# A 576 KB broadcast for the MLP gate moves from GpSimd's DMA queue beside the last transpose to SyncE's queue behind fc1's weights

## Chip, cores, metric

One core of a Trainium2 chip. The metric is device microseconds of one execution. The kernel before ran in 248.44 us (median of 3, 248.24 to 248.64) when the prediction was made.

## The reference, cut to what matters

```python
B, N, D = (2, 256, 1152); F = 4 * D                 # bf16 throughout
mod = (_silu(c) @ w_mod).reshape(B, 6, 1, D)
shift_a, scale_a, gate_a, shift_m, scale_m, gate_m = [mod[:, i] for i in range(6)]
...                                                  # attention, x = x + gate_a * a
h2 = _layernorm(x) * (1 + scale_m) + shift_m
m = _gelu(h2 @ w_fc1) @ w_fc2
return x + gate_m * m
```

`gate_m` is needed only when fc2's results are evicted, at the end. The kernel computes it on VectorE: it loads the sixth section of `w_mod` transposed, and multiplies it with silu(c), repeated on all 128 partitions. That repeated copy of silu(c), `s_all`, is the load that moves.

## The kernel before

Four blocks matter: the LayerNorm ahead of the MLP, whose rows are transposed by DMA; fc1's first eight column blocks, in two halves by batch; the broadcast; and what uses it.

```python
def ln2_transpose(t):                                   # four of these, SyncE's queue
    nc.sync.dma_start_transpose(hT[:, :, t * P:(t + 1) * P], xn2[t][:])
...
ln2_normalize(3, 5 * P)
ln2_transpose(3)                                        # the last one

w_f1[1] = load_panels("w_f1_1", wfc1_v, D)              # SyncE's queue, nine loads of 864 KB
w_f1[2] = load_panels("w_f1_2", wfc1_v, 2 * D)
w_f1[3] = load_panels("w_f1_3", wfc1_v, 3 * D)
w_gate_mT = wide_tile("w_gate_mT")
for r in range(0, KD, 3):
    nc.sync.dma_start_transpose(w_gate_mT[...], w_mod[...])
...                                                     # cut
MSPLIT = 8
for b in range(B):                                      # batch 0 needs transposes 0, 1; batch 1 needs 2, 3
    for m0 in range(0, MSPLIT, 2):
        pacc = acc_tile([P, 2, N], "pacc")
        for m in (m0, m0 + 1):
            for k in range(KD):
                f1_mm(pacc[:, m - m0, :], m, k, b * N, (b + 1) * N)
        if b == 0 and m0 == MSPLIT - 2:
            ln2_modulate(1)                             # nine modulations of hT, VectorE and ScalarE
        nc.scalar.activation(gT[:, m0:m0 + 2, b * N:(b + 1) * N], pacc[:], ACT.Gelu_apprx_tanh)
late = act.tile([P, NT, D], BF16, name="late", tag="x_in")   # takes the buffer of x_sb
s_all = late[:, 0:B, :]
for b in range(B):
    nc.gpsimd.dma_start(s_all[:, b, :], s_dram[b:b + 1, :].partition_broadcast(P))
...                                                     # cut
for m in range(MSPLIT, KF):                             # the other 28 column blocks, 512 wide
    ...
    if m == 14:
        dot_section(w_gate_mT, s_all, late[:, B, :], gcol)   # 18 multiply-and-sum passes on VectorE
        gate_m = gate_m_finish()
```

The program order of the text is not the time of the load. GpSimd's last work before it ends at 99.03 us, and what is left to wait for is the buffer of x_sb. The trace has the broadcast issued at 101.12 us, after 2.09 us of idling that VectorE's last LayerNorm statistics ended; the fourth transpose follows at 103.24 us.

## Time and profile before

| | before |
|---|---|
| median, three runs | 248.44 us |
| span of the trace, mean granted clock | 247.1 us, 0.993 |
| fourth transpose, issue to landing | 4.99 us |
| PE's wait ahead of fc1's batch-1 half | 2.21 us |
| stretch at half clock behind it | 3.41 us |
| dot passes start / first fc2 eviction | 145.65 / 183.89 us |

The lines behind these numbers, and how they are read, are in the prediction.

### The profile page before, as it was taken

The page shows a single profiled execution, that of the slowest core. Times are in us where ns is not written, and L with a number is a line of the kernel's source. Part 1 is how long each engine was busy: PE and PEld are TensorE (multiplying, and loading weights), DVE is VectorE, ACT ScalarE, POOL GpSimd, SP SyncE. Part 2 cuts the span into 40 slices and gives each one's busy share as a digit, 9 for nine tenths or more (in the row PEclk, how much of TensorE's full clock was granted, in tenths as well). Part 3 has the DMA queues.
Part 4 walks back from the last instruction along what each step waited for, and adds up shares of the span by engine and source line. Part 5 has one row for each costly group of instructions (what it writes and reads, how often), then busy time and mean ns, then how long its engine had stood idle before and what let it go on. Part 6 is the DMA issues. An engine that isn't in the chain of part 4 may idle for free.

```text
span 247.1 us, 3879 instructions
## 1 busy us (share of the span) xinstructions
PE 237.8 (96%) x1637; PEld 140.1 (57%) x1648; DVE 84.7 (34%) x198; ACT 65.5 (27%) x127; POOL 31.8 (13%) x48
## 2 busy tenths in 40 slices
PE   6999999999999999969999999999999999999994
PEld 2585444465666666848544444444566666666673
DVE  3752462115625768520000049997011000000001
ACT  6632350133514155752322233222000000000000
POOL 1000012000311515200000000002031222111111
PEclk9999999999999999997999999999999999999999
DMA  6999999999999951599999999996950000000000
GB/s 227 326 336 362 366 327 312 371 353 344 338 309 346 330 117 20 108 267 327 326 327 221 218 279 329 327 326 184 335 162 32 16 19 16 16 20 17 31 16 19
DMA packets 70685, 53.89 MB, mean 218 GB/s; under 512 B 18939, under 2 KB 65419, under 8 KB 70667
## 3 DMA queue, kind: packets, MB, share of 16 engines
q1 hardware_dynamic: 69776, 51.84, 71.8%
q0 software_dynamic: 864, 1.79, 2.6%
q8 instruction: 13, 0.21, 0.4%
q14 instruction: 5, 0.04, 0.0%
q10 hardware_dynamic: 27, 0.00, 0.0%
HBM read 48.08 MB, written 1.19 MB: 199 GB/s over the span
## 4 chain that ended last, share of the span: by engine, by line
PE 87%; DMA 5%; DVE 4%; ACT 1%; issue 1%; SPq 0%; DVEq 0%; ACTq 0%
PE pacc L766 29%; PE pacc L702 26%; PE pacc L503 7%; PE pacc L438 7%; PE pacc L612 5%; PE pk L253 4%; DMA w_scale_a<-in_w_mod_dram 3%; PE pk L282 2%; DMA hT<-xn 2%; PE pn L365 1%; PE ps_s L458 1%; PE pa L530 1%; DVE stats L624 1%; DVE stats L163 1%; PE pm L221 1%
## 5 line engine op out<-in xcount | busy, mean ns | idle before, releaser
L702 PE MATMUL pacc<-hT,w_f 128*128 128x512 bf16 (+1 forms) x390 | 72.1, 346 | 2.5 <-DVE hT L599 2.2
L766 PE MATMUL pacc<-w_f,gT 128*128 128x384 bf16 (+2 forms) x468 | 70.5, 314 | 0.1
L702 PEld LDWEIGHTS <-w_f 128*128 128x128 bf16 x396 | 39.5, 100 | 34.9 <-issue 2.9
L766 PEld LDWEIGHTS <-gT 128*128 128x128 bf16 x468 | 44.4, 98 | 26.2
L429 DVE SCALAR_TENSOR_TENSOR late<-w_gate_mT,late 128x1152 bf16<-128x1152 bf16 x18 | 24.4, 1358 | 36.3 <-DMA w_gate_mT<-in_w_mod_dram 35.7
L772 DVE TENSOR_TENSOR tmp<-pacc,gate 128x384 f32<-128x384 f32 (+2 forms) x13 | 6.9, 528 | 65.8 <-PE pacc L766 53.3
L743 ACT ACTIVATE gT<-pacc 128x512 bf16<-128x512 f32 x28 | 16.7, 597 | 37.7 <-PE pacc L702 36.3
L774 POOL TENSOR_TENSOR o_sb<-tmp,x 128x384 bf16<-128x384 f32 (+1 forms) x12 | 11.7, 973 | 50.8 <-DVE tmp L772 50.8
L612 PE MATMUL pacc<-w_o,big 128*128 128x384 bf16 (+2 forms) x117 | 18.1, 314 | 0.0
L503 PE MATMUL pacc<-w_v,hT 128*128 128x384 bf16 x108 | 17.9, 326 | 0.0
L438 PE MATMUL pacc<-hT,w_q 128*128 128x512 bf16 x80 | 17.6, 379 | 0.1
L612 PEld LDWEIGHTS <-big 128*128 128x128 bf16 x117 | 10.9, 98 | 7.1 <-DVE big L270 0.6
L503 PEld LDWEIGHTS <-hT 128*128 128x128 bf16 x108 | 10.4, 98 | 7.2 <-issue 0.5
L253 PE MATMUL pk<-big,w_k 128*128 128x256 bf16 (+2 forms) x88 | 13.3, 292 | 0.5 <-ACT big L240 0.4
L438 PEld LDWEIGHTS <-w_q 128*128 128x128 bf16 x81 | 7.9, 98 | 9.6
L618 POOL TENSOR_TENSOR x<-tmp,x_sb 128x384 f32<-128x384 f32 x10 | 9.1, 911 | 17.9 <-DVE tmp L617 10.8
L420 POOL DMA_DIRECT2D gates_dram<-grow x4 | 2.0, 512 | 69.3 <-DVE grow L729 69.3
L253 PEld LDWEIGHTS <-w_k 128*128 128x128 bf16 x90 | 7.5, 97 | 3.4 <-DMA w_k<-in_wqkv_dram 0.3
L617 DVE TENSOR_TENSOR tmp<-pacc,gate 128x384 f32<-128x384 f32 (+2 forms) x13 | 6.7, 519 | 4.8 <-PE pacc L612 4.7
L146 PE MATMUL pwarm<-zeros 128*128 128x512 bf16 x18 | 7.1, 560 | 1.2 <-DVE eps_t L92 1.2
L420 POOL DMA_DIRECT2D s_dram<-s_rows x4 | 2.6, 654 | 34.5 <-DVE s_rows L423 34.5
L240 ACT ACTIVATE big<-pt,scale_a 128x256 bf16<-128x256 bf16 (+1 forms) x12 | 4.6, 434 | 9.0 <-PE pt L231 7.4
(97 smaller groups left out, 151.2 us busy)
## 6 DMA issues: line engine op xcount, KB each, us to landing
w_f<-in_w_fc_dram SPq DMA_DIRECT2D x14, 864.0 KB, 11.1
w_f<-in_w_fc_dram SPq DMA_DIRECT2D x2, 2592.0 KB, 10.5
w_f<-in_w_fc_dram SPq DMA_DIRECT2D x2, 1728.0 KB, 13.2
w_shift_a<-in_w_mod_dram SPq DMA_DIRECT2D x3, 864.0 KB, 11.4
w_q<-in_wqkv_dram SPq DMA_DIRECT2D x3, 864.0 KB, 12.0
w_v<-in_wqkv_dram SPq DMA_DIRECT2D x3, 864.0 KB, 10.5
w_gate_a<-in_w_mod_dram SPq DMA_DIRECT2D x3, 864.0 KB, 9.9
w_o<-in_wo_dram SPq DMA_DIRECT2D x3, 864.0 KB, 13.8
```

Of the source, the lines that this page charges most:

```text
L146: nc.tensor.matmul(dst[:], zeros[:, 0:P], zeros[:], start=True, stop=True)
L253: nc.tensor.matmul(pk[m][:, c0:c1], w_k[:, k, m * P:(m + 1) * P], hT0[:, k, c0:c1], start=(k == 0 and c0 == 0), stop=(k == KD - 1), skip_g ...
L429: nc.vector.scalar_tensor_tensor(spill, wT[:, j, :], 1.0, s_all[:, b, :], op0=ALU.mult, op1=ALU.mult, accum_out=dst[:, b * KD + j:b * KD + ...
L438: nc.tensor.matmul(pacc[:], w_q[:, k, m * P:(m + 1) * P], hT[:, k, :], start=(k == 0), stop=(k == KD - 1),)
L503: nc.tensor.matmul(pacc[:], hT[:, k, t * P:(t + 1) * P], w_v[:, k, pnl * PW:(pnl + 1) * PW], start=(k == 0), stop=(k == KD - 1),)
L612: nc.tensor.matmul(pacc[:], aT[:, k, t * P:(t + 1) * P], w_o[:, k, c0:c1], start=(k == 0), stop=(k == KD - 1),)
L618: (nc.gpsimd if i < 2 or t % TPB == 0 else nc.vector).tensor_tensor(x1[:, t, c0:c1], tmp[:], x_sb[:, t, c0:c1], op=ALU.add)
L702: nc.tensor.matmul(dst, w_f1[m // KD][:, k, ml * P:(ml + 1) * P], hT[:, k, c0:c1], start=(k == 0), stop=(k == KD - 1),)
L743: nc.scalar.activation(gT[:, m, :], pacc[:], ACT.Gelu_apprx_tanh)
L766: nc.tensor.matmul(pacc[:], gT[:, kk, t * P:(t + 1) * P], w_f2[j][:, r, c0 - n * PW:c0 - n * PW + cw], start=(kk == 0), stop=(kk == KF - 1),)
L772: nc.vector.tensor_tensor(tmp[:], pacc[:], gate_m[:, b, c0:c0 + cw], op=ALU.mult)
L774: (nc.vector if last else nc.gpsimd).tensor_tensor(o_sb[:], tmp[:], x1[:, t, c0:c0 + cw], op=ALU.add)
```

## The change

The intent is to take the broadcast's traffic away from the transpose that PE waits for, and to put it where PE waits for nothing that comes by DMA. SyncE issues its DMAs in program order, so there it comes behind fc1's last weights.

```diff
     w_f1[3] = load_panels("w_f1_3", wfc1_v, 3 * D)
+    late = act.tile([P, NT, D], BF16, name="late", tag="x_in")
+    s_all = late[:, 0:B, :]
+    for b in range(B):
+        nc.sync.dma_start(s_all[:, b, :], s_dram[b:b + 1, :].partition_broadcast(P))
     w_gate_mT = wide_tile("w_gate_mT")
@@ behind fc1's two halves
-    late = act.tile([P, NT, D], BF16, name="late", tag="x_in")
-    s_all = late[:, 0:B, :]
-    for b in range(B):
-        nc.gpsimd.dma_start(s_all[:, b, :], s_dram[b:b + 1, :].partition_broadcast(P))
```

## The prediction

> **What bounds the kernel now.** I read the page's first and fourth parts first: TensorE matmuls are busy 96% of the 247.1 us span and 87% of the chain that ended last is PE, so a change to a 576 KB load can only matter where PE waits for it, directly or through something that it slows. The slices of the page have one place where the granted clock falls, the eighteenth to nineteenth (about 111 to 117 us).
>
> ```profile
> PE 237.8 (96%) x1637; PEld 140.1 (57%) x1648; DVE 84.7 (34%) x198; ACT 65.5 (27%) x127; POOL 31.8 (13%) x48
> PEclk9999999999999999997999999999999999999999
> ```
>
> Then the waits of PE: the longest of the whole kernel is a single one of 2.2 us in front of fc1's second half (batch 1, line 702), released by the modulation of hT on VectorE. The chain in order of time says what lies behind it.
>
> ```profile
> 102.29 0.93 ACT xn L577
> 103.22 0.02 issue
> 103.24 4.99 DMA hT<-xn
> ...
> 108.32 0.36 DVE hT L599
> 108.68 0.04 issue
> 108.72 10.42 PE pacc L702 x73
> ```
>
> So the last of the four DMA transposes of the normalised rows is on the path, 4.99 us from issue to landing. The view of the tile hT gives all four; at least two, and by the view of the DMA queues in short stretches three, took 3.2 us:
>
> ```profile
> DMA to landing us min/median/max: 3.2/3.2/5.0
> ```
>
> The timelines of GpSimd and PE around it show what ran beside the slow one, and the hole:
>
> ```profile
> 101.12 1.08 POOL L721 DMA_DIRECT2D late<-s_dram  x2 [2.09 <-DVE stats L624]
> ```
> ```profile
> 98.48 8.02 PE L702 MATMUL pacc<-hT,w_f 128*128 128x256 bf16 x72
> 108.72 3.68 PE L702 MATMUL pacc<-hT,w_f 128*128 128x256 bf16 x19 [2.21 <-DVE hT L599]
> ```
>
> The two broadcasts of 288 KB are issued at 101.1 and 101.7 and land 5.2 and 5.5 us later, at about 106.4 and 107.2. In quarter-microsecond windows the DMA engines fall back at 102.75 (the third transpose's bytes are through), then stay at 110 to 280 GB/s until 106.5. The fourth transpose, issued at 103.24, moves its bytes in the middle of that. The third, issued at 100.28, was done as the broadcast's bytes began, and took 3.2 us. That is the evidence that the broadcast is what costs the fourth 1.8 us.
>
> The hole has a second price. Windows of PE behind it:
>
> ```profile
> 108.72:110.34 1.62, 1.62 (x11) 0.97 (x11) 1.23 (x5) 1.62 (x4) 0.00 (x0) 1.00 1.08 332
> 110.34:113.75 3.41, 3.41 (x19) 2.35 (x17) 0.00 (x0) 0.63 (x2) 0.00 (x0) 0.51 1.09 328
> 113.75:119.14 5.39, 5.39 (x48) 4.67 (x48) 0.00 (x0) 1.37 (x3) 0.00 (x0) 1.00 1.10 326
> ```
>
> The columns are the stretch, its length, busy time and count of PE, weight loads, VectorE, ScalarE and GpSimd, then the granted clock. For 3.41 us the clock is half. The second half of this stage (73 matmuls) thus takes 10.42 us, where 72 of the first half took 8.02, or 8.13 for 73: 2.29 us longer, of which 3.41 x 0.5 = 1.71 is the clock and the remaining 0.58 the start at the pace of the nine modulations.
>
> **What the Trainium skill says.** "DMA: Bandwidth & Descriptors", section "Issuing engines are not separate DMA queues": transfers started by GpSimd, Sync or Scalar all run on the same 16 DMA engines and interleave. The trace agrees: a transpose on SyncE's queue took 4.99 instead of 3.2 us beside GpSimd's load. The same page, "DMA Transpose (X-bar)" and "Rules for kernel authors": a transpose next to ordinary DMAs needs no serialising, so I expect no new forced wait from putting the broadcast directly ahead of the gate's transposes; no run of before has that order. "TensorE: Matmul & The Clock Gate", Part 1: the clock gate watches PE activity in free-running windows of 3413 ns and drops to half after an idle window. The trace agrees with the length (3.41 us at half clock) and with the half, but it differs on the condition: the idle stretch was 2.21 us, not a whole window, and was followed by a thinly filled start. So what counts seems to be how full a window was, and the measurement decides.
>
> **The change part by part.** The instruction order of the changed program shows the same instructions on every engine but for two: GpSimd loses the two broadcasts, and SyncE has them between fc1's fourth quarter and the three transposes of w_gate_mT. PE, VectorE and ScalarE keep their order. The two copies wait there for the writers of s_dram, for x_sb's last reader on GpSimd, and for older transfers that share their semaphores, all long past.
> - *Removed:* the traffic beside the fourth transpose. It then should take what the other three do, 3.2 us: 103.24 + 3.2 = 106.44 instead of 108.22, 1.79 us less. The first modulation follows 0.10 later and takes 0.36, then 0.04 to PE: 106.94. PE ends the first half at 98.48 + 8.02 = 106.50, so the hole shrinks from 2.21 to 0.43 us. It doesn't close, so the whole 1.79 us are gained on the path.
> - *The clock:* with a hole of 0.43 and the 0.58 of the paced start, a window of 3.41 us loses about 1.0 us and is some 70% filled. Before, the worst window (107.00 to 110.41) had PE busy for 1.69 of 3.41 us, 50%, and was followed by the drop. The start of the kernel has thin windows too: 10.00 to 13.41 has 2.66 of 3.41, 78%, without a drop. The new 70% lies between; I put 85% on no drop. Gain if so: 1.71 us; expected 1.45.
> - *Added on SyncE's queue:* 2 x 288 KB, some 590 kB at the 327 GB/s that the loads run at, 1.8 us of the DMA engines around 127 us. The gate's transposes (issued from 127.25 on), the dot passes that wait for them (145.65) and fc2's first loads (143.60) move back by up to about 2 us. Is any of it on the path? First use of the gate: the dot passes start at 145.65 and the first fc2 eviction at 183.89, 38.24 us behind, so it moves to some 186.
>
> ```profile
> 145.65 1.36 DVE L429 SCALAR_TENSOR_TENSOR late<-w_gate_mT,late 128x1152 bf16<-128x1152 bf16 x1 [35.70 <-DMA w_gate_mT<-in_w_mod_dram]
> 183.89 0.56 DVE L772 TENSOR_TENSOR tmp<-pacc,gate 128x384 f32<-128x384 f32 x1 [12.59 <-DMA gate<-gates_dram]
> ```
>
> PE has six accumulators and needs 70.47 / 12 = 5.87 us for one group of fc2, so from a start at 169.6 it would first stall at 169.6 + 6 x 5.87 = 204.9: 19 us of slack. VectorE catches up at 0.56 us a group, GpSimd at about 1.0. fc2's first weights, issued at 143.60, take 10.6 us (landing 154.2), the second panel's about 13 (near 160); 2 us later both are still 7 us or more ahead of 169.6. None of this is on the path.
> - *Sum:* 1.79 + 1.71 = 3.50 us when both come, 1.79 when the clock still drops. 248.44 - 3.50 = 244.94; weighted, 248.44 - 1.79 - 1.45 = 245.2. I take 245.1.
>
> **The rivals.**
> 1. *The clock drops all the same.* The windows are free-running, so how the hole lies in them can decide. For it: 70% is below the fullest thin window that I can show as harmless. The time would be 246.6.
> 2. *w_fc1's second quarter takes the broadcast's place.* Its loads are issued behind the fourth transpose at 104.63, and bytes follow about 1.1 us after an issue here (transpose issued 90.64, engines active from 91.75): from 105.75. The undisturbed transpose moves its bytes from about 104.35 to 106.0, so the overlap is 0.3 us or so. If the slow 4.99 us were mostly this load's doing, the gain would be a few tenths: 248.0. Against it: the engines are visibly at work from 103 on, before those loads are even issued. A partial overlap, landing at 3.6 us, costs 0.4: 245.4.
> 3. *The gate comes late, or fc2's weights do.* SyncE's queue is in order, so a copy that had to wait would hold back the transposes and all fc2 loads behind it. The slack of 7 and 19 us speaks against it; it would need a wait of over 7 us to show, and then the time would exceed 248.4.
>
> **Range and chances.** Both gains give 244.9, a partly disturbed transpose without the drop 245.4, the drop 246.6 to 247. Runs of before lie within 0.2 us of the median. Eight in ten: 244.4 to 246.9. The gain can't reach the 2% line (243.47) unless more than hole and clock went: the two together, hole closed, are 2.21 + 1.71 = 3.92, leaving 244.5. Faster by over 2%: 0.02; slower: 0.01; within: 0.97.
>
> **What would show it.** Right: the fourth transpose lands in 3.2 to 3.6 us; PE's wait ahead of the second half is 0.4 to 0.8 us; no window at half clock near 110 us; fc1's full-width part starts near 115.7 instead of 119.19; the dot passes start 0 to 2.5 us later, PE never waits in fc2. Wrong: a transpose that still takes about 5 us (rival 2), a half clock behind a short hole (rival 1), or a wait of PE at line 766 or for w_fc1 panels (rival 3).

## The result, and the profile after

The changed kernel took 245.33 us (median of 4, 245.28 to 246.9) against 248.54 us (median of 4) for the kernel before; the ratio is 0.9887, 95% interval 0.9847 to 0.9928. (A ratio is the mean time of one kernel's fast runs over that of the other's fast runs of the same rounds, so not quite the ratio of the medians.) The change is a gain of 1.1%, real but within the 2% line.

First the chain in order of time of the kernel after: start, duration, what.

```profile
103.68 0.93 ACT xn L577
104.61 0.02 issue
104.63 3.29 DMA hT<-xn
...
108.02 0.36 DVE hT L599
108.37 0.04 issue
108.41 8.76 PE pacc L706 x73
```

The fourth transpose takes 3.29 instead of 4.99 us, and the 73 matmuls behind it 8.76 instead of 10.42. The timeline of PE has the hole shrunk from 2.21 to 0.50 us, and the windows behind it stay at full clock (columns as in the prediction):

```profile
99.89 8.02 PE L706 MATMUL pacc<-hT,w_f 128*128 128x256 bf16 x72
108.41 11.78 PE L706 MATMUL pacc<-hT,w_f 128*128 128x256 bf16 x86 [0.50 <-DVE hT L599]
```
```profile
110.03:113.44 3.41, 3.41 (x34) 3.05 (x32) 0.00 (x0) 1.01 (x3) 0.00 (x0) 1.00 1.10 332
```

In these 3.41 us 31 matmuls began where 16 began before (the views' counts, 34 and 19, take in the three that were already running).

One thing must not be read as an effect of the change. All times in this trace up to the hole are 1.4 us later than before (fc1 starts at 99.89, not 98.48): this profiled run was the 246.9 us one, and its slices of granted clock show why:

```profile
PEclk9889999999999999999999999999999999999999
```

The clock fell early, at about 10 to 14 us, in code that is the same in both kernels, behind a PE wait of 1.2 us for the first weights. The other three runs had mean granted clocks of 0.998 to 1.0 and took 245.3. So in the first four runs each, after had a half clock in one run of four, at another place; before had one in its profiled run and, by their times (248.2 us and more, see below), in the other three, whose clocks are not listed. Comparing two traces by absolute time would hide 1.4 us of the gain; comparing each stage by its own length does not.

### The profile page after: what moved, and what is told of

It is laid out like the page before. It is cut to its first block, busy times and chain, and to the rows that moved or that the text cites. A ratio compares the mean times of both kernels' runs of the same rounds, so it can differ in the third digit from the quotient of the medians.

```text
span 245.0 us, 3884 instructions
## 1 busy us (share of the span) xinstructions
PE 237.3 (97%) x1637; PEld 140.3 (57%) x1648; DVE 84.5 (34%) x198; ACT 65.5 (27%) x127; POOL 30.7 (13%) x46
## 4 chain that ended last, share of the span: by engine, by line
PE 89%; DMA 4%; DVE 4%; issue 1%; ACT 1%; SPq 0%; DVEq 0%; ACTq 0%
PE pacc L766 29%; PE pacc L706 25%; PE pacc L503 7%; PE pacc L438 7%; PE pacc L612 6%; PE pk L253 5%; DMA w_scale_a<-in_w_mod_dram 3%; PE pk L282 2%; PE pn L365 1%; PE ps_s L458 1%; PE pa L530 1%; DMA hT<-xn 1%; PE pt L231 1%; DVE stats L624 1%; PE pm L221 1%
## 5 line engine op out<-in xcount | busy, mean ns | idle before, releaser
L706 PE MATMUL pacc<-hT,w_f 128*128 128x512 bf16 (+1 forms) x390 | 70.5, 340 | 0.8 <-DVE hT L599 0.5
L706 PEld LDWEIGHTS <-w_f 128*128 128x128 bf16 x396 | 38.6, 98 | 32.4 <-issue 1.2
L253 PE MATMUL pk<-big,w_k 128*128 128x256 bf16 (+2 forms) x88 | 14.2, 311 | 0.5 <-ACT big L240 0.4
L253 PEld LDWEIGHTS <-w_k 128*128 128x128 bf16 x90 | 8.4, 107 | 3.5 <-issue 0.5
```

Source lines behind the costliest of these rows:

```text
L253: nc.tensor.matmul(pk[m][:, c0:c1], w_k[:, k, m * P:(m + 1) * P], hT0[:, k, c0:c1], start=(k == 0 and c0 == 0), stop=(k == KD - 1), skip_g ...
L706: nc.tensor.matmul(dst, w_f1[m // KD][:, k, ml * P:(ml + 1) * P], hT[:, k, c0:c1], start=(k == 0), stop=(k == KD - 1),)
```

## The experiments

Each run lists its mean granted clock, which makes two groups of the runs of one kernel: below 0.996 (a stretch of half clock somewhere) and above. I give both where it matters. The theory at the start: (a) the broadcast's traffic slows the transpose, 1.8 us; (b) the hole that this opens makes the clock drop, 1.7 us more. The rivals: it is the queue or the descriptor generator and not the traffic; the second weight quarter's load, which follows 1.3 us behind the transpose, is the disturber; the new place costs something.

### The changed kernel again, for the spread

> The changed kernel unaltered, for the spread. Its first four runs were 246.9, 245.28, 245.35 and 245.32 us, and the profiled one, 246.9, had a half clock between some 12 and 20 us, before anything that the change touches, and a PE wait of 1.2 us for the first weights. If that early drop is chance, most runs lie at 245.3 and a few at 246.9; the profile here then mostly has no such drop, a last transpose of 3.2 to 3.4 us, a hole of about 0.5 us and no half clock at fc1. If the change brought the early drop with it, it shows again in most runs, and never in the kernel before.

245.45 us (median of 6; 245.13 to 246.47), before beside it 248.2 (median of 11), ratio 0.9903, interval 0.9873 to 0.9933. One run of six had an early half clock, again the profiled one; its fourth transpose took 3.26 us, its hole was 0.48 us. A third set of its runs, beside the last experiment, is called the repeat below. The surprise is in the kernel before: five of its eleven runs had clocks of 0.997 or more and took 246.95 to 247.64, the six others 248.2 to 249.0. So the half clock of before is not certain, as its first runs had made it seem.

### The load kept on GpSimd's queue, but later

```diff
+    hold = small.tile([P, 2], BF16, name="hold", tag="hold", bufs=1)
+    nc.gpsimd.tensor_copy(hold[:], gT[:, MSPLIT - 1, T - 2:T])   # waits for fc1's last half-width GELU
     late = act.tile(...)                                          # then as before, nc.gpsimd.dma_start
```

> The kernel before with the two broadcasts still on GpSimd's queue, but held until fc1's last half-width GELU (a two-column copy of gT on GpSimd ahead of them). Theory (traffic beside the last transpose costs): the last transpose lands in 3.2 to 3.4 us, the hole is about 0.5 us, no half clock at fc1, time within 0.3 us of the changed kernel, 245.3. Rival (it matters which queue or generator carries the load): a time near the kernel before, 248.5. Rival (something else of the change): in between.

245.53 us (245.26 to 245.81, six runs), ratio 0.9902: the changed kernel's time within 0.1 us. The transpose took 3.24 us, the hole 0.47 us, no run had a half clock.

```profile
103.08 3.24 DMA hT<-xn
```

GpSimd's queue by itself costs nothing; what counts is when the load runs.

### No load at all (wrong result)

```diff
-        nc.gpsimd.dma_start(s_all[:, b, :], s_dram[b:b + 1, :].partition_broadcast(P))
+        nc.gpsimd.memset(s_all[:, b, :], 0.0)
```

> The kernel before without the broadcast at all: GpSimd clears the tile instead, so the MLP gate is zero and the result is wrong on purpose. It bounds what any placement of the load can be worth. Theory: the same 3.2 us transpose, 0.5 us hole and clock as the changed kernel, 245.3 within 0.3 us, so that the new place on SyncE's queue is free. Rival (the new place costs something that the old place's removal hides): clearly below the changed kernel, 244.8 or less.

245.57 us (245.37 to 246.37, four runs), transpose 3.33 us, hole 0.55 us. Nothing is left to gain from this load: the new place is free within the spread. It also answers the rival of the second weight quarter: those loads are issued just as before, 1.3 us behind the transpose, and alone they leave it at 3.3 us.

### The same traffic from ScalarE's queue

```diff
     ln2_normalize(3, 5 * P)
+    for b in range(B):                     # late and s_all allocated here; the changed kernel's two
+        # copies on SyncE's queue are taken out
+        nc.scalar.dma_start(s_all[:, b, :], s_dram[b:b + 1, :].partition_broadcast(P))
     ln2_transpose(3)
```

> The broadcasts issued from ScalarE's queue right behind the last normalisation, so at the moment the last transpose is issued from SyncE's: hardware queue, but the same traffic beside the transpose. Theory (traffic): the transpose lands in 4.5 to 6 us, the hole is 1.7 us or more, probably with the half clock behind it: 247.5 to 249. Rival (it is GpSimd's software-made descriptors that slow the transpose): 3.2 to 3.5 us to landing and some 245.5, allowing for the two issues on ScalarE.

The transpose took 5.06 us, the hole was 2.28 us. Three runs at clocks of 0.991 and 0.992 took 248.65 to 248.98, one at 1.0 took 247.01; ratio to before 1.0011 (0.995 to 1.0072). This is the kernel before over again from another engine's queue.

```profile
103.18 5.06 DMA hT<-xn
```

The Trainium skill, "DMA: Bandwidth & Descriptors", section "Issuing engines are not separate DMA queues", has the DMAs of all issuing engines run on the same 16 DMA engines. The trace agrees: the transpose takes 5.06 us beside ScalarE's load and 4.99 beside GpSimd's.

### The load on SyncE's queue just ahead of the transpose

```diff
     ln2_normalize(3, 5 * P)
+    for b in range(B):                     # late and s_all allocated here; the changed kernel's two
+        # copies behind fc1's weights are taken out
+        nc.sync.dma_start(s_all[:, b, :], s_dram[b:b + 1, :].partition_broadcast(P))
     ln2_transpose(3)
```

> The broadcasts on SyncE's queue just ahead of the last transpose instead of behind fc1's fourth quarter: issued near 101.6 us, when the third transpose's issue is over, some 1.6 us before the last transpose. Their bytes should run from about 102.8 to 104.6 at 327 GB/s, where the last transpose's own begin near 104.4. If only overlap in time counts, the transpose takes 3.2 to 3.8 us and the time is 245.3 to 245.9. If the queue's order holds the transpose's start back (two issues of 0.5 to 1 us and their waits), it is issued late by some tenths up to 2 us: 245.6 to 248.5.

A miss. The transpose was issued on time (103.28 us) but took 4.63 us; 246.91 us in the one run without a half clock, 247.8 to 248.38 with one, ratio 0.9991 (0.9946 to 1.0037). I had let the broadcast's 590 kB run at the weights' 327 GB/s, 1.8 us. In the packets of the trace they last from 102.75 to some 106.2 us, 3.4 us. The same is true of the kernel before; its view of the DMA queues from 103 to 106.6 us (packets, MB, share of the 16 engines):

```profile
q0 software_dynamic: 158, 0.59, 64.3%
q1 hardware_dynamic: 464, 0.11, 41.9%
```

0.59 MB in 3.6 us is 164 GB/s: this load holds the engines for twice as long as its bytes suggest, and an early issue of 1.6 us does not get it out of the way.

How that reaches the transpose is seen in the same view cut in three, on SyncE's queue q1 of the kernel before (103 to 105, 105 to 106.5, 106.5 to 107.75 us), and in one cut of the repeat of the changed kernel (103.9 to 105.9 us):

```profile
q1 hardware_dynamic: 28, 0.00, 0.8%
...
q1 hardware_dynamic: 425, 0.11, 98.7%
...
q1 hardware_dynamic: 864, 0.26, 90.4%
```
```profile
q1 hardware_dynamic: 1202, 0.31, 87.3%
```

By the packet records of the trace a transpose is 1,152 packets of 256 bytes; the other packets in these counts are 4-byte completion writes and, at the end, the first of the next weights. Alone, all 1,152 go between 104.2 and 105.8 us. Beside the broadcast not one of them moves before 105.1 us, 421 move until 106.5, and the other 731 go in a burst, most of it within 0.9 us, as soon as the broadcast is gone. So the transpose isn't slowed in proportion; it stands until some 60% of the other load's packets have begun. Why it stands so long is not shown. The length of the broadcast's packets (the twelve longest took 0.5 to 0.9 us each) can't be all of it: from ScalarE's queue they took at most 0.51 us, and there the transpose's first packet moved even later, at 105.73 us.

The 28 packets of q1 in the first cut are completion writes of the third transpose. The semaphore updates in the packed trace put its landing at 105.6 us, 5.3 us after its issue, where in the changed kernel it took 3.2. So the broadcast holds up two transposes; only the later one is on the path.

### Distinct source rows in place of the broadcast (wrong result)

```diff
-        nc.gpsimd.dma_start(s_all[:, b, :], s_dram[b:b + 1, :].partition_broadcast(P))
+        nc.gpsimd.dma_start(s_all[:, b, :], w_mod[b * P:(b + 1) * P, 0:D])
```

> The kernel before with the two loads at the old place and queue, of the same size, but each partition reads its own row of w_mod instead of all reading one row of s_dram (wrong result on purpose). In the trace of before the broadcast's packets take up to 0.9 us each and its 590 kB run from 103.0 to 106.5, some 170 GB/s. If it is the shared source row that makes the load slow, distinct rows run at about 330 GB/s, are through by about 105, and the transpose lands in 3.5 to 4.2 us: 245.5 to 246.5. If any 590 kB from GpSimd's queue cost the same, it takes 5.0 us: 247.3 or 248.7 by the clock.

Mostly a miss. The transpose took 4.39 us. Two runs without a half clock took 246.58 and 247.01, two with one 248.6 and 248.72; ratio 0.9971 (0.993 to 1.0011). By this one profile the shared source row accounts for 0.6 of the 1.7 us; most of the delay comes also from a load of the same size with distinct rows. That load was hardly faster itself: 0.59 MB in the view of 103.2 to 106.3 us, 190 GB/s, and not the 330 that I had expected.

### Eight dummy matmuls in the hole of the kernel before

```diff
     for b in range(B):
+        if b == 1:
+            warm(8, acc_tile([P, T], "pwarm3"))      # 512 wide, operands are the zeros tile
         for m0 in range(0, MSPLIT, 2):
```

> The kernel before with eight dummy 512-wide matmuls (8 x 0.219 = 1.75 us at full clock) between fc1's two half-width halves, where PE otherwise sits idle for 2.2 us; the broadcast stays beside the transpose. Theory of two separate prices: the transpose still lands in 5.0 us and the second half still starts at the same point, but the half clock of 3.41 us is gone, so 248.5 - 1.7 = 246.8. Rival (the half clock comes from elsewhere or the second half is slow for another reason, such as operands arriving): no change, 248.5.

A plain miss: 250.07 us (248.8 to 250.63), ratio 1.0082. The transpose took 6.39 us in its profile, 1.4 us longer than in before, with the same broadcast beside it, and four of the six runs had a half clock all the same (0.991 to 0.993). So it could not separate the two prices, and it raised a question: can PE's work slow a DMA?

### Nine column blocks in halves, on top of the change

```diff
-    MSPLIT = 8
+    MSPLIT = 9
...
-            for m in (m0, m0 + 1):
+            m1 = min(m0 + 2, MSPLIT)               # the ninth block has an accumulator of its own
+            for m in range(m0, m1):
```

> The changed kernel with nine instead of eight of fc1's column blocks done in two batch halves, all from the first weight quarter: the first half is 9 more matmuls of 256 columns, about 1.0 us, longer and covers the rest of the wait for the last transpose and part of the nine modulations. Theory: the hole of 0.5 us is gone and so is most of the 0.58 us of paced start, at a cost of 18 x 0.111 - 9 x 0.219 = 0.03 us: 0.5 to 1.0 us less than the changed kernel, 244.3 to 244.8. Rival (the load of the second quarter or the slot of the first is then late): no gain or a wait for weights in fc1, 245.3 or more.

Two runs took 244.98 and 245.09, as the theory had it; three took 246.15 to 246.2, all at full clock, and one 247.81 at 0.993. In the profiled run (246.19) the fourth transpose took 5.19 us and PE waited 1.44 us, though no broadcast was near. Its view of the DMA queues from 106 to 107.3 us, first, and that of the changed kernel's repeat for the same stretch:

```profile
DMA packets 346, 0.28 MB, mean 213 GB/s; under 512 B 8, under 2 KB 345, under 8 KB 345
...
q1 hardware_dynamic: 345, 0.26, 76.8%
q8 instruction: 1, 0.02, 4.2%
```
```profile
DMA packets 392, 0.30 MB, mean 232 GB/s; under 512 B 0, under 2 KB 392, under 8 KB 392
```

At 106.15 us one packet of 16 KB of the instruction queue took 0.88 us of one DMA engine. The transpose's data were through by then (the last six of the eight small packets in the view), but its last two completion writes, of 4 bytes each, came at 107.02 us instead of 105.8. The packed trace has sixteen completion updates for each transpose: here fifteen had come by 3.54 us after the issue, and the last at 5.19. The failed experiment of the eight dummies has such a fetch too, at 107.74 us: there two completion writes came at 108.7 us, and fifteen updates had come by 4.84 us, the last at 6.39. In the kernel before, and in the changed one, the fetch falls at 111 to 113 us, behind the transpose. The Trainium skill has this in "Runtime: NRT & Kernel Launch", section "Instruction fetch mechanics": the sequencer refills its instruction memory in blocks of 16 KiB, 256 instructions, over a DMA queue of its own. The trace agrees with 13 such packets in a run, about one for every 256 of the 3,285 matmuls and weight loads. More PE instructions ahead of the hole, or none to stop PE's sequencer at it, bring the fetch forward. This is a theory of its own, and the next three runs test it.

### Four dummy matmuls instead of eight

```diff
-            warm(8, acc_tile([P, T], "pwarm3"))
+            warm(4, acc_tile([P, T], "pwarm3"))
```

> The kernel before with four dummy matmuls (0.88 us) in the hole instead of eight. With eight, an instruction fetch of 16 KB fell on the tail of the transpose (one packet of some 0.95 us at 107.7 us) and the transpose landed in 6.4 us. Theory: with eight instructions fewer PE's sequencer comes to the fetch only behind the hole, so it is at 109 us or later and the transpose lands in about 5.0 us again; a window then has PE busy for about 2.6 instead of 1.7 of 3.41 us, so fewer runs than before's ten of eighteen have a half clock, and those without lie at 247.3 as before's do: a median near 247.4. Rival (dummy matmuls themselves slow the transpose, by their reads of SBUF): the transpose takes clearly over 5.0 us with no fetch near it, 248.5 to 250.

Confirmed. 247.44 us (246.86 to 247.92, six runs) against 248.8 for before (median of 11), ratio 0.9958 (0.9933 to 0.9983). The fetch is at 112.8 us, the transpose took 4.96 us as in before, and none of the six runs had a half clock, where eight of the eleven of before had one. The timeline of PE (the dummies are line 146):

```profile
106.71 1.03 PE L146 MATMUL pwarm<-zeros 128*128 128x512 bf16 x3
109.06 13.28 PE L702 MATMUL pacc<-hT,w_f 128*128 128x256 bf16 x93 [1.32 <-DVE hT L599]
```

So these dummies do not slow the transpose. And this is the clean test of price (b): 0.88 us of dummy work, which brings nothing forward, gains 1.36 us by medians and 1.1 by means, and its runs (mean 247.42 us) are as fast as those of before without a half clock (247.36). Its worst stretch of 3.41 us among those I cut has PE busy for 2.04 us, 60%.

### Nine blocks, with the instruction stream shifted

```diff
-    warm(14, pwarm)
+    warm(5, pwarm)
+    for _ in range(40):
+        nc.tensor.matmul(pwarm[:, 0:32], zeros[:, 0:P], zeros[:, 0:32], start=True, stop=True)
```

> The kernel with nine column blocks in halves, with nine of the early 512-wide warm-up matmuls replaced by forty 32-wide ones of about the same total time: 62 more PE instructions, so each later instruction fetch comes about 62 instructions earlier. In the kernel without this shift a 16 KB fetch at 106.15 us fell on the tail of the last transpose, which landed in 5.2 us. Theory: the fetch moves by some 3 us, off that tail, the transpose lands in 3.2 to 3.4 us and the full gain appears: most runs at 244.7 to 245.1, none of the 246.2 kind. Rival (PE's nine more matmuls, not the fetch, slow the transpose): 5.2 us again, 246.2 in most runs. The start may also lose its warm clock, which the clock of the first 20 us would show.

245.7 us (245.47 to 246.16). The fetch moved forward to 103.65 us, where it hit the third transpose: by the semaphore updates in the packed trace it landed 4.7 us after its issue. (The view's largest, 5.2 us, is the first transpose, beside the fetch before, at 91.51 us: fifteen of its updates had come by 3.6 us, the last at 5.2.) The fourth took 3.3 us with PE busy throughout: fc1 has no wait at all. But the time did not fall to 245, because the narrow matmuls ran at 30 ns each and were over too soon: PE then waited 3.24 us for the first weights, and three of the six runs had a half clock, the profiled one early. The mechanism was as expected; the filler was not.

### Nine blocks, shifted by 50 instructions, and the changed kernel beside it

```diff
     warm(14, pwarm)
+    for _ in range(25):
+        nc.tensor.matmul(pwarm[:, 0:32], zeros[:, 0:P], zeros[:, 0:32], start=True, stop=True)
```

> Nine column blocks in halves, with 25 narrow (32-wide) matmuls added behind the fourteen early warm-ups, 50 PE instructions, and nothing taken away. The shift by 62 instructions moved the fetch from 7.84 to 3.77 us behind fc1's start, onto the third transpose; 50 should put it at some 4.6 us behind, about 102.9, between the bytes of the third transpose (to 102.75) and those of the fourth (from 104.25). The narrow ones took some 30 ns each at full clock, 0.75 us in all, and fit into the wait of 1.0 us for the first weights. Theory: both transposes land in about 3.2 us, PE has no hole at fc1, and the time is 244.6 to 245.1 in most runs, below the changed kernel's 245.4. Rival (the fetch still hits one of them, or the start is longer): 245.4 or more.

> The changed kernel once more, beside the last one on the same chip, since the two should differ by 0.3 to 0.8 us only: 245.1 to 245.7, with an occasional run near 246.5 that has an early half clock.

245.06 us (244.56 to 245.24, five runs) against 245.29 (245.16 to 245.97, four runs) for the changed kernel and 248.55 for before; ratios to before 0.9858 (0.9827 to 0.9888) and 0.9877 (0.9845 to 0.9908). The fetch came 4.66 us behind fc1's start, where I had put it at 4.6. PE's work in fc1 has no wait in it; the third transpose took 3.4 us and the fourth 3.3. None of the five runs was of the 246.2 kind, as three of six were without the shift:

```profile
98.98 23.27 PE L708 MATMUL pacc<-hT,w_f 128*128 128x256 bf16 x185
```

This version lies 0.4 us of the means below the changed kernel, but the ranges overlap, so that it is the faster of the two is not shown; and it depends on where a fetch falls, which edits of PE's instruction stream move again. I would keep the changed kernel's form unless the last half microsecond is wanted.

## Why the prediction was right

Right in time (245.1 predicted, 245.33 measured, range 244.4 to 246.9) and in direction and size (gain 3.4 predicted, 3.2 measured). The closeness is in part luck: over all runs whose clock is listed, 38 of before and 14 of the changed kernel, the means are 248.31 and 245.57 us, a gain of 2.7. Step by step:

- **The transpose.** Predicted 3.2 us alone and a gain of 1.79 us on the path; the fourth measured 3.24 to 3.33 us whenever no broadcast ran beside it and no fetch fell on it. Taking only runs without a half clock, before has 247.36 us (mean of 12 whose clock is listed) and after 245.39 (12 runs), 1.97 us apart. Shown, both ways: traffic back from another queue brings 5.06 us back; the old queue at a later time does not. One reading behind it was wrong: the prediction has the third transpose done in 3.2 us when the broadcast's bytes begin. Its data were through, but it landed after 5.3 us, so it too was held up. The conclusion gains by that.
- **The hole.** Predicted 0.43 us, measured 0.47 to 0.55.
- **The clock.** Predicted 1.71 us, with 85% on no drop in the changed kernel. The mechanism was right, and is shown by the four dummy matmuls. The size was off in two ways. Before does not always have the drop: 26 of the 38 runs with a listed clock did. And it costs 1.39 us (248.75 against 247.36), not 1.71. The likely reason for the latter is that the half clock can begin before PE is back at full pace: in the run with ScalarE's queue it began near 109.4 us, during the paced start, and not at 110.3. That was read off one trace and not tested.

  When the drop comes is told in part by the clock's changes in the packed traces. In each they lie whole multiples of 3.413 us apart (in before 7.98 and 110.38 us, thirty of them), and against the start of the program the grid is shifted from run to run. The stretch of the grid that held the hole had PE busy for 1.66 us of 3.41 in before, 1.14 with ScalarE's queue and 1.83 with distinct rows, and a drop came at its end. With SyncE ahead the hole of 1.85 us was cut by the grid, 2.62 and 2.35 us busy on its two sides, and no drop came. The line is not sharp: 1.89 us with eight dummies had none, 1.98 at the start of the changed kernel's first profiled run had one. So where the grid falls is the likely reason that some runs of before have the drop and others not; no run tests it.

  The average share of the clock in the gain is then 26/38 of 1.39, about 0.95 us, of which the changed kernel gives a little back: 2 of its 14 runs had a half clock, both profiled ones early in the kernel. The first runs of before, which by their times all had the drop, made the sum of 3.50 fit better than it should have.
- **The added traffic.** Predicted to move the dot passes back by up to 2 us, off the path. They did not move: in the repeat, whose start was undisturbed, they begin at 145.42, before at 145.65. The term was mis-sized. The gate's three transposes start 1.2 us later in the repeat (128.42 against 127.25) but were issued in 14.81 us instead of 16.25; that they now meet less of fc1's loads is the likely reason, not a tested one. The conclusion held: PE has no wait in fc2, and the missing load gains nothing more.
- **Rivals.** The half clock all the same: not seen at this place in any of the three profiles of the changed kernel. The second weight quarter as disturber: it isn't, by the run without the load, though with the broadcast ahead of it the transpose's rest shares its last 0.5 us with it. A late gate: the first fc2 eviction is at 183.41 in the repeat, as harmless as before.

The prediction had a blind spot that cost it nothing: instruction fetches on the DMA engines. They decided two of the experiments.

## What to carry to other kernels

A DMA queue whose engine is idle can issue long before the place where the text puts it (here at 101.12 us, ahead of the fc1 half that precedes it in the text and starts at 108.72); look for what else is in flight at that moment, and move bulk loads away from a transfer that PE waits for. What such a wait costs is its length and, for some runs, a stretch of half clock behind it, so read the granted clock of every run before comparing times, and compare runs of the same clock. When a small edit of PE's instruction stream changes a transfer that it should not touch, look for an instruction fetch beside it.

## What the Trainium skill lacked or had wrong

- "TensorE: Matmul & The Clock Gate", Part 1, asks for an idle window of about 3.4 us before the clock drops, and "Why this matters for your kernels" warns of gaps over about 3 us. The page also has a case of many short idle stretches, but no figure of how full a window must be. Here a gap of 2.21 us with a thin start behind it was enough in 26 of 38 runs (worst window 50% busy); with 0.88 us of it filled (60%), none of 6. Whether it drops also varies from run to run of one program.
- "DMA: Bandwidth & Descriptors", "Queues, rings and completion order", has the queues take turns packet by packet; the trace shows how uneven that can be (whether its packets are the page's is not shown): none of the transpose's 256-byte packets moved in the 0.7 us or so after its usual start, 1.1 us behind its issue, beside packets of up to 0.9 us, and none in 1.4 us beside ScalarE's, of up to 0.51 us. Its landing went from 3.2 to 5.0 and 5.1 us.
- The same page gives no rate for a load that repeats one row on 128 partitions. Here it ran at 164 GB/s beside a transpose (0.59 MB in 3.6 us), the weights at about 327. But distinct rows in the same place ran at 190 only, so the repeated row is the smaller part of the loss.
- "Runtime: NRT & Kernel Launch", "Instruction fetch mechanics", calls the cost of a fetch mostly hidden. It lacks what the fetch does to others: each 16 KB packet took 0.9 to 1.7 us of one shared DMA engine, and one beside a transpose's tail moved its landing to 5.2 us, when fifteen of its sixteen completion updates had come by 3.54.
